# Every second step's second stage in three float32r passes on high and low parts

## The chip, the cores and the metric

The kernel runs on one core of a Trainium2 chip. The metric is the device time of one execution in microseconds (us); three runs of the kernel before gave 1559.08, 1560.92 and 1562.91 us, with the median 1560.92. Profiles are of single executions.

## The reference

The input x has 8 batches of 3136 rows and 256 columns. Each column is filtered over the rows by a real Fourier transform, a product with a complex filter and the transform back. The result goes through a gated feed-forward stage: a product with w_in (256 to 1024), a maximum with zero, a convolution of width 3 along the rows, a sigmoid of it as a gate, and a product with w_out (1024 to 256).

```python
X = np.fft.rfft(x, axis=1)
F = (filt_r + 1j * filt_i)[None, :, :]
y = np.fft.irfft(X * F, n=x.shape[1], axis=1)

h = np.maximum(y @ w_in, 0.0)
...
gate = 1.0 / (1.0 + np.exp(-conv_out))
out = (h * gate @ w_out)
```

## The kernel before

The transform of length 3136 is factored as 112 x 28 and written as matrix products. It is done in steps: 14 steps for each of 8 batches, 112 in all; step number m stands for batch m // 14 and p = m % 14. As 14 is even, p is even where m is even. A step holds two of the 28 sub-transforms, as tiles of about 112 partitions and 2 x 256 elements. What happens to a step, by the functions of the kernel:

- `load` brings x from memory (SyncE's queue), `first` multiplies by s1 on TensorE (8 matmul records, L323), and `keep` copies the result from PSUM into the tile `turn` on ScalarE (L327). These run a whole batch ahead of the rest.
- `turn` transposes a part of the kept tiles on TensorE (L334), and `turned_rows` copies the result `ps` from PSUM to the tile `a` on ScalarE (L339).
- `second` multiplies `a` by s2 on TensorE in plain float32 into `pp` (L346; the last step of a batch in two halves, L349). A float32 matmul shows as two records.
- `filt` multiplies by the filter on VectorE, three instructions that read `pp` from PSUM (L358 to L360), and adds the two products `u` and `v` into `z` on GpSimd (L362).
- `third` multiplies `z` by i1 on TensorE (L233), and `store` copies the result on ScalarE (L237) and writes it to memory.
- `last_stage` and `last_out` read it back, multiply by m2 (L215) and split the result into a high float32r part on ScalarE (`hi_act`, L146) and a low one, the difference, on VectorE (`lo_dve`, L149). For batch 0 this stands at the end of the transform (i from 113); for the others it is spread over the feed-forward stage.

The order of the four compute engines is written out by hand: `manual_schedule` keeps each engine to the order of the code. One iteration i, with m = i - 15, does in this order: `last_out` (late iterations only), `filt(m-2)`, `third(m-4)`, `first(i-1)`, `second(m-1)`, `turn(m)`, `store(m-4)`, `keep(i-1)`, `turned_rows(m)`, `copy_filter` (the first 14 steps), one piece of the weight conversion, `last_stage`. So `a` of step m is written in iteration i, behind `turn(m)`, and read in iteration i + 1, behind `third` and `first`; and on VectorE stands in one iteration `filt(m-2)`, then the conversion.

The weight conversion (`to_f32`, L160 to L174) makes float32 of float64 words for w_in and w_out. From i = 36 on, `next(wsteps)` advances it by one call in each iteration, by two where i is a multiple of 8. Of ten calls, seven issue one VectorE operation between tiles in SBUF (128x512 each), the others work on GpSimd and ScalarE.

PSUM has eight buffers in the transform: five named `ps`, used in turn by `first`, `turn`, `third` and `last_stage`, and three named `pp`. `mm3` (L176 to L179) is the helper for a product in three passes: high x high, high x low, low x high. The feed-forward stage uses it for w_in, and starts when batch 0 is split as a whole.

Of the kernel before, what the change touches and what calls it, by code (L numbers as in the profile page):

```python
# [9 lines left out]
F32 = mybir.dt.float32  # L10
F32R = mybir.dt.float32r
I32 = mybir.dt.int32
U32 = mybir.dt.uint32
AF = mybir.ActivationFunctionType
# [6 lines left out]
D = 256  # L21
# [103 lines left out]
def tile_fft_filter_gated_ffn(  # L125
# [16 lines left out]
    nc = tc.nc  # L142
    B = x.shape[0]

    def hi_act(dst, src):
        nc.scalar.activation(dst, src, AF.Copy)  # L146

    def lo_dve(dst, src, hi):
        nc.vector.tensor_tensor(out=dst, in0=src, in1=hi.bitcast(F32), op=ALU.subtract)  # L149
# [26 lines left out]
    def mm3(ps, wh, wl, rh, rl, start=True, stop=True, **kw):  # L176
        nc.tensor.matmul(ps, lhsT=wh, rhs=rh, start=start, stop=False, **kw)  # L177
        nc.tensor.matmul(ps, lhsT=wh, rhs=rl, start=False, stop=False, **kw)  # L178
        nc.tensor.matmul(ps, lhsT=wl, rhs=rh, start=False, stop=stop, **kw)  # L179
# [16 lines left out]
    def last_load(b, c):  # L196
        br = lp.tile([112, 2, D], F32, name="br", bufs=4)
        nc.sync.dma_start(out=br, in_=b_dram[b][c:c + 2].rearrange("n p d -> p n d"))
        lasts[b, c] = br
# [18 lines left out]
    def last_out(b, c):  # L218
        yh, yl = y_slices(b, slice(c, c + 2))
        pv = lasts.pop((b, c))[:, 0:4 * N1].rearrange("p (k c a) -> p k c a", c=2, a=N1)  # L220
        hi_act(yh, pv)
        lo_dve(yl, pv, yh)

    NP = 14
# [5 lines left out]
    def third(b, p, ps):  # L230
        z = parts.pop((b, p))
        for j in range(2):
            nc.tensor.matmul(ps[:, j], lhsT=i1_sb[:, 2 * p + j], rhs=z[:, j], start=True, stop=True)  # L233

    def store(b, p, ps):
        st = rest.tile([112, 2, D], F32, name="sb")
        nc.scalar.activation(st, ps, AF.Copy)  # L237
        v = b_dram[b].rearrange("n (r g) d -> (n r) g d", g=G)
        nc.scalar.dma_start(out=v[:, 2 * p:2 * p + 2], in_=st)
# [5 lines left out]
    with (  # L245
# [6 lines left out]
        eye_sb = fc.tile([128, 128], F32, name="eye_sb")  # L252
        s2_sb = fc.tile([112, 120], F32, name="s2_sb")
        s2s_sb = fc.tile([112, 120], F32, name="s2s_sb")

        turned = [fc.tile([120, 2, D], F32, name=f"v{k}") for k in range(2)]
        for v in turned:
# [7 lines left out]
        def load_filter(p):  # L265

            sl = slice(2 * p, 2 * p + 2)
            nc.sync.dma_start(out=t2_sb[0:56, sl], in_=fi[0:56, sl])
            nc.sync.dma_start(out=t1_sb[64:120, sl], in_=fr[64:120, sl])
            if p == NP - 1:  # L270
                nc.sync.dma_start(out=t1_sb[0:56, sl], in_=fr[0:56, sl])
            nc.sync.dma_start(out=i1_sb[:, sl], in_=i1[:, sl])

        def copy_filter(p):
            sl = slice(2 * p, 2 * p + 2)
            nc.scalar.activation(t2_sb[64:120, sl], t2_sb[0:56, sl], AF.Copy, scale=-1.0)
            if p < NP - 1:
                nc.vector.tensor_copy(t1_sb[0:56, sl], t1_sb[64:120, sl])
# [38 lines left out]
        def first(b, p):  # L317

            r = rows.pop(("x", b, p))
            ps = fps.tile([128, 512], F32, name="ps")[:, 0:448].rearrange("p (k n m) -> p k n m", k=KT, n=2)  # L320
            for j in range(2):
                for k in range(KT):
                    nc.tensor.matmul(ps[:, k, j], lhsT=r[:, j, 128 * k:128 * k + 128], rhs=s1_sb[:, 2 * p + j], start=True, stop=True)  # L323
            return ps

        def keep(b, p, ps):
            nc.scalar.activation(turns[b % 2][:, :, 2 * p:2 * p + 2], ps, AF.Copy)  # L327

        def turn(b, p):
            ps = fps.tile([112, 2, D], F32, name="ps")  # L330
            for j in range(2):
                for k in range(KT):
                    v = turns[b % 2][:, k].rearrange("p n (r g) -> p (n r) g", g=G)[:, :, 2 * p + j]
                    nc.tensor.transpose(ps[:, j, 128 * k:128 * k + 128], v, eye_sb)  # L334
            return ps

        def turned_rows(b, p, ps):
            r = fp.tile([112, 2, D], F32, name="a", bufs=2)
            nc.scalar.activation(r, ps, AF.Copy)  # L339
            rows["a", b, p] = r  # L340

        def second(b, p):
            r = rows.pop(("a", b, p))
            pp = fps.tile([120, 2, D], F32, name="pp", bufs=3)
            if p < NP - 1:
                nc.tensor.matmul(pp, lhsT=s2_sb, rhs=r, start=True, stop=True)  # L346
            else:
                for j, m in ((0, s2_sb), (1, s2s_sb)):
                    nc.tensor.matmul(pp[:, j], lhsT=m, rhs=r[:, j], start=True, stop=True)  # L349
            psums[b, p] = pp  # L350

        def filt(b, p):


            pp, v = psums.pop((b, p)), turned[p % 2]
            sl = slice(2 * p, 2 * p + 2)
            u = fp.tile([120, 2, D], F32, name="u")
            nc.vector.tensor_mul(u, pp, t1_sb[:, sl])  # L358
            nc.vector.tensor_mul(v[64:120], pp[0:56], t2_sb[0:56, sl])  # L359
            nc.vector.tensor_mul(v[0:56], pp[64:120], t2_sb[64:120, sl])  # L360
            z = rest.tile([120, 2, D], F32, name="z")
            nc.gpsimd.tensor_tensor(out=z, in0=u, in1=v, op=ALU.add)  # L362
            parts[b, p] = z

        def at(i):
            return divmod(i, NP) if 0 <= i < NP * B else None
# [4 lines left out]
        def load_first(i):  # L371
            if i < NP and i % 2 == 0:
                nc.sync.dma_start(out=s1_sb[:, 2 * i:2 * i + 4], in_=s1[:, 2 * i:2 * i + 4])
            if bp := at(i):
                load(*bp)
# [7 lines left out]
        with tc.manual_schedule(engines=COMPUTE):  # L383
            for i in range(NI):
                m = i - SKEW
                if i == done:
                    assert next(wsteps, None) is None
                    convert_pools.close()
                    forward_pools.close()
                    yps.append(ctx.enter_context(tc.tile_pool(name="y_even", bufs=1, side="right", reuse_waits="tile")))  # L390
                    lp = ctx.enter_context(tc.tile_pool(name="lp", bufs=2, side="right", reuse_waits="tile"))
                if i:
                    load_first(i + XBUFS - 1)
                if i == 8:
                    nc.sync.dma_start(out=eye_sb, in_=eye)
                    nc.sync.dma_start(out=s2_sb, in_=s2[:, 0:120])
                    raws["cw"] = cv.tile([128, 6 * NF], I32, name="rawc", bufs=1)
                    nc.sync.dma_start(out=raws["cw"], in_=conv_w)
                if 10 <= i < 10 + NP:
                    load_filter(i - 10)  # L400
                if i == 16:
                    nc.sync.dma_start(out=s2s_sb, in_=s2s[:, 0:120])
                    nc.sync.dma_start(out=m2_sb, in_=m2)
                c = 2 * (i - done)
                if 0 <= c - 4 < N2:
                    last_out(0, c - 4)
                if bp := at(m - 2):
                    filt(*bp)
                pt = None
                if (bp := at(m - 4)) and m - 4 <= END:  # L410
                    pt = fps.tile([112, 2, D], F32, name="ps")
                    third(*bp, pt)
                pf = first(*bp) if (bp := at(i - 1)) else None
                if bp := at(m - 1):
                    second(*bp)
                pa = turn(*bp) if (bp := at(m)) else None
                if pt is not None:
                    store(*at(m - 4), pt)
                if pf is not None:
                    keep(*at(i - 1), pf)  # L420
                if pa is not None:
                    turned_rows(*at(m), pa)
                if 0 <= m - 1 < NP:
                    copy_filter(m - 1)
                if 14 <= i < 22:
                    next(csteps, None)
                if i in (30, 32):
                    load_weights((i - 30) // 2)
                if i >= 36:
                    for _ in range(2 if i % 8 == 0 else 1):  # L430
                        next(wsteps, None)
                if 0 <= c - 2 < N2:
                    last_stage(0, c - 2, fps.tile([128, 512], F32, name="ps"))
                if 0 <= c < N2:
                    last_load(0, c)
# [156 lines left out]
```

## Time and profile before

| | |
|---|---|
| median of three runs | 1560.92 us |
| the profiled execution, its own time | 1562.36 us |
| its span, first to last instruction | 1560.6 us |
| PE busy share | 99% |
| DVE busy share | 83% |
| ACT busy share | 80% |
| POOL busy share | 45% |
| mean granted TensorE clock | 0.999 |
| share of the chain of waits: PE, DVE, DMA, ACT | 92%, 4%, 2%, 1% |

PE is TensorE, PEld its weight loads, DVE VectorE, ACT ScalarE, POOL GpSimd, SP SyncE. A group's row gives the line of the kernel, the engine, the operation, the tile written and those read, the shape, the count, the busy time in us with the mean of one in ns, and behind the last bar the idle time of the engine before such instructions and who ended it. A timeline's row begins with the start and the duration in us; in square brackets stands the idle time before. A row of the chain of waits has start, duration and what was waited for. Matmuls are pipelined: the start of the next one tells what a matmul costs, not its own length.

### The profile page before, as it was taken

Reading aid. Unit: us, or ns where it says so; the run is one execution under the profiler, and the core shown is the slowest. Engines: PE = TensorE matmul, PEld = TensorE weight load, DVE = VectorE, ACT = ScalarE, POOL = GpSimd, SP = SyncE. Lnnn points to the kernel's source line nnn. Section 1 sums busy time; section 2 is a strip of 40 time slices with the busy share of each in tenths; the row PEclk is TensorE's granted clock in tenths of the full one; section 3 lists DMA queues with packets and bytes.
Section 4 is the critical chain, followed back from the end, with each engine's and each line's share of the span. In section 5 each row is a group of like instructions: output and inputs, shape, how many; then the busy total and the mean of one; then the engine's idle time right before and its main releaser. Section 6 shows DMA issues by size and latency. Waiting matters only on the chain.

```text
span 1560.6 us, 27784 instructions
## 1 busy us (share of the span) xinstructions
PE 1539.0 (99%) x10320; PEld 1418.8 (91%) x10320; DVE 1294.3 (83%) x1978; ACT 1245.1 (80%) x2274; POOL 703.9 (45%) x625
## 2 busy tenths in 40 slices
PE   8999999998999999999999999999999999999998
PEld 7778777777999999999999999999999999999998
DVE  3788888788888888888888888888888888888887
ACT  5655555666888888888888888888888888888887
POOL 2455555543444444444444444444444444444444
PEclk9999999999999999999999999999999999999999
DMA  9865655442111011111111011111011110100001
GB/s 228 253 184 165 181 166 162 138 143 88 31 54 48 30 48 48 48 49 48 48 42 34 27 54 48 48 48 48 31 45 46 49 54 26 47 25 24 25 25 48
DMA packets 89062, 115.24 MB, mean 74 GB/s; under 512 B 7400, under 2 KB 60168, under 8 KB 88928
## 3 DMA queue, kind: packets, MB, share of 16 engines
q1 hardware_dynamic: 74592, 87.77, 18.5%
q10 hardware_dynamic: 14336, 25.70, 5.8%
q8 instruction: 82, 1.34, 0.3%
q14 instruction: 52, 0.43, 0.1%
HBM read 62.06 MB, written 51.38 MB: 73 GB/s over the span
## 4 chain that ended last, share of the span: by engine, by line
PE 92%; DVE 4%; DMA 2%; ACT 1%; issue 0%; POOL 0%; SPq 0%; ACTq 0%; POOLq 0%
PE ps_h L178 12%; PE ps_h L179 12%; PE ps_h L177 11%; PE po L494 11%; PE po L496 11%; PE po L495 11%; PE ps_h L215 6%; PE ps L323 5%; PE ps L233 5%; PE pp L346 5%; PE ps L334 2%; DVE y L149 1%; DMA x<-in_x 1%; DVE v L360 1%; DVE v L359 1%; DVE u L358 1%
## 5 line engine op out<-in xcount | busy, mean ns | idle before, releaser
L152 POOL TENSOR_TENSOR g<-t,g 128x448 fp32r<-128x448 f32 x448 | 517.7, 1156 | 663.1 <-ACT g L146 259.6
L494 PE MATMUL po<-wo,g 128*128 128x256 f32 x1568 | 441.5, 282 | 0.0
L496 PE MATMUL po<-wo,g 128*128 128x256 f32 x1568 | 433.8, 277 | 0.0
L495 PE MATMUL po<-wo,g 128*128 128x256 f32 x1568 | 433.4, 276 | 0.0
L468 DVE SCALAR_TENSOR_TENSOR t<-ps_h,cw,t 128x448 f32<-128x448 f32 x448 | 305.5, 682 | 84.6 <-ACT t L463 73.8
L178 PE MATMUL ps_h<-y,wi 128*128 128x450 f32 x896 | 330.4, 369 | 5.2 <-DVE y L149 5.2
L177 PE MATMUL ps_h<-y,wi 128*128 128x450 f32 x896 | 329.1, 367 | 3.9 <-DVE t L474 2.6
L179 PE MATMUL ps_h<-y,wi 128*128 128x450 f32 x896 | 328.8, 367 | 0.0
L469 DVE SCALAR_TENSOR_TENSOR t<-ps_h,cw,t 128x448 f32<-128x448 f32 x448 | 306.4, 684 | 16.0
L463 ACT ACTIVATE t<-ps_h,cw 128x448 f32<-128x448 f32 x448 | 285.2, 637 | 41.5 <-ACT ps_h L461 0.4
L494 PEld LDWEIGHTS po<-wo,g 128*128 128x128 f32 x1568 | 294.8, 188 | 7.0
L495 PEld LDWEIGHTS po<-wo,g 128*128 128x128 f32 x1568 | 294.3, 188 | 5.7
L496 PEld LDWEIGHTS po<-wo,g 128*128 128x128 f32 x1568 | 294.5, 188 | 0.0
L461 ACT ACTIVATE ps_h<-ps_h 128x450 f32<-128x450 f32 x448 | 251.5, 561 | 33.6 <-PE ps_h L179 27.7
L474 DVE TENSOR_TENSOR t<-ps_h,t 128x448 f32<-128x448 f32 x448 | 275.2, 614 | 0.1
L473 ACT ACTIVATE t<-t 128x448 f32<-128x448 f32 x448 | 255.0, 569 | 12.0 <-DVE t L469 10.8
L146 ACT ACTIVATE g<-t 128x448 fp32r<-128x448 f32 x448 | 254.4, 568 | 0.2 <-DVE t L474 0.2
L362 POOL TENSOR_TENSOR z<-u,v 120x512 f32<-120x512 f32 x112 | 156.8, 1400 | 186.2 <-DVE v L360 166.3
L178 PEld LDWEIGHTS ps_h<-y,wi 128*128 128x128 f32 x896 | 168.4, 188 | 14.3 <-DVE y L149 7.5
L177 PEld LDWEIGHTS ps_h<-y,wi 128*128 128x128 f32 x896 | 170.0, 190 | 12.3 <-DVE t L474 3.8
L179 PEld LDWEIGHTS ps_h<-y,wi 128*128 128x128 f32 x896 | 168.3, 188 | 13.9
L149 DVE TENSOR_TENSOR y<-ps_h,y 128x448 fp32r<-128x448 f32 x98 | 103.2, 1053 | 76.9 <-ACT y L146 76.9
(62 smaller groups left out, 1660.9 us busy)
## 6 DMA issues: line engine op xcount, KB each, us to landing
x<-in_x SPq DMA_DIRECT2D x112, 224.0 KB, 3.1
b_dram<-sb ACTq DMA_DIRECT2D x112, 224.0 KB, 3.2
br<-b_dram SPq DMA_DIRECT2D x112, 224.0 KB, 2.6
out<-ot SPq DMA_DIRECT2D x27, 896.0 KB, 4.1
raw<-in_w_in SPq DMA_DIRECT2D x8, 256.0 KB
raw<-in_w_out SPq DMA_DIRECT2D x8, 256.0 KB
t_sb<-in_fr SPq DMA_DIRECT2D x15, 112.0 KB
t_sb<-in_fi SPq DMA_DIRECT2D x14, 112.0 KB
```

The costliest lines, as they stand in the source:

```text
L152: nc.gpsimd.tensor_tensor(out=dst, in0=src, in1=hi.bitcast(F32), op=ALU.subtract)
L177: nc.tensor.matmul(ps, lhsT=wh, rhs=rh, start=start, stop=False, **kw)
L178: nc.tensor.matmul(ps, lhsT=wh, rhs=rl, start=False, stop=False, **kw)
L179: nc.tensor.matmul(ps, lhsT=wl, rhs=rh, start=False, stop=stop, **kw)
L463: nc.scalar.activation(t, h[:, 1:SUB + 1], AF.Copy, scale=cw[:, 1, f:f + 1])
L468: nc.vector.scalar_tensor_tensor(out=t, in0=h[:, 0:SUB], scalar=cw[:, 0, f:f + 1], in1=t, op0=ALU.mult, op1=ALU.add)
L469: nc.vector.scalar_tensor_tensor(out=t, in0=h[:, 2:SUB + 2], scalar=cw[:, 2, f:f + 1], in1=t, op0=ALU.mult, op1=ALU.add)
L473: nc.scalar.activation(t, t, AF.Sigmoid)
L474: nc.vector.tensor_mul(t, h[:, 1:SUB + 1], t)
L494: nc.tensor.matmul(o, lhsT=gh[:, sl], rhs=wo[0][:, f], start=first, stop=False, skip_group_check=True)
L495: nc.tensor.matmul(o, lhsT=gh[:, sl], rhs=wo[1][:, f], start=False, stop=False, skip_group_check=True)
L496: nc.tensor.matmul(o, lhsT=gl[:, sl], rhs=wo[0][:, f], start=False, stop=last, skip_group_check=True)
```

## The change

In even steps ScalarE's copy of the turned rows is replaced by `hi_act`, which writes a float32r tile `a_hi` of the same shape, and VectorE gets a new instruction, `lo_dve`, which writes `a_lo`, the difference of the PSUM tile and `a_hi`. `second` then runs three float32r passes with s2, split in the same way once at i = 12, in place of a float32 matmul. Odd steps keep the float32 form, the last step of a batch (p = 13) with its two halves too. The buffers of `a` are one each of `a`, `a_hi` and `a_lo` in place of two of `a`.

```diff
+        s2_parts = [fc.tile([112, 120], F32R, name=f"s2_{h}") for h in ("hi", "lo")]
...
         def turned_rows(b, p, ps):
-            r = fp.tile([112, 2, D], F32, name="a", bufs=2)
-            nc.scalar.activation(r, ps, AF.Copy)
+            if p % 2:
+                r = fp.tile([112, 2, D], F32, name="a", bufs=1)
+                nc.scalar.activation(r, ps, AF.Copy)
+            else:
+                r = [fp.tile([112, 2, D], F32R, name=f"a_{h}", bufs=1) for h in ("hi", "lo")]
+                hi_act(r[0], ps)
+                lo_dve(r[1], ps, r[0])
             rows["a", b, p] = r
...
-            if p < NP - 1:
+            if p % 2 == 0:
+                mm3(pp, *s2_parts, *r)
+            elif p < NP - 1:
                 nc.tensor.matmul(pp, lhsT=s2_sb, rhs=r, start=True, stop=True)
...
+                if i == 12:
+                    hi_act(s2_parts[0], s2_sb)
+                    lo_dve(s2_parts[1], s2_sb, s2_parts[0])
```

Where the instructions stand now, at three places. In the kernel after the change the lines are shifted: L366 to L368 are the filter's three products, L335 the turn, L324 the first stage, L354 the float32 second stage.

On VectorE, in the iterations with the weight conversion (`em`, `ws` and `raw` are its tiles); before:

```order
L164 TENSOR_TENSOR em<-em 128x512
L358 TENSOR_TENSOR u<-pp,t_sb 120x512
L359 TENSOR_TENSOR v_102<-pp,t_sb 56x512
L360 TENSOR_TENSOR v_102<-pp,t_sb 56x512
L166 TENSOR_SCALAR em<-raw 128x512
L358 TENSOR_TENSOR u<-pp,t_sb 120x512
L359 TENSOR_TENSOR v_103<-pp,t_sb 56x512
L360 TENSOR_TENSOR v_103<-pp,t_sb 56x512
L168 SCALAR_TENSOR_TENSOR ws<-em 128x512
```

The same stretch now:

```order
L164 TENSOR_TENSOR em<-em 128x512
L366 TENSOR_TENSOR u<-pp,t_sb 120x512
L367 TENSOR_TENSOR v_104<-pp,t_sb 56x512
L368 TENSOR_TENSOR v_104<-pp,t_sb 56x512
L149 TENSOR_TENSOR a_lo<-ps,a_hi 112x512
L166 TENSOR_SCALAR em<-raw 128x512
L366 TENSOR_TENSOR u<-pp,t_sb 120x512
L367 TENSOR_TENSOR v_105<-pp,t_sb 56x512
L368 TENSOR_TENSOR v_105<-pp,t_sb 56x512
L168 SCALAR_TENSOR_TENSOR ws<-em 128x512
```

In every second iteration the low part stands between the filter and the conversion; the other iterations are as they were.

On VectorE, in the last iterations of the transform, where batch 0's output is split (`y`); before:

```order
L149 TENSOR_TENSOR y_3322<-ps,y_3321 128x2x2x112
L358 TENSOR_TENSOR u<-pp,t_sb 120x512
L359 TENSOR_TENSOR v_103<-pp,t_sb 56x512
L360 TENSOR_TENSOR v_103<-pp,t_sb 56x512
L149 TENSOR_TENSOR y_3322<-ps,y_3321 128x2x2x112
```

Now:

```order
L367 TENSOR_TENSOR v_104<-pp,t_sb 56x512
L368 TENSOR_TENSOR v_104<-pp,t_sb 56x512
L149 TENSOR_TENSOR a_lo<-ps,a_hi 112x512
L149 TENSOR_TENSOR y_3526<-ps,y_3525 128x2x2x112
L366 TENSOR_TENSOR u<-pp,t_sb 120x512
L367 TENSOR_TENSOR v_105<-pp,t_sb 56x512
L368 TENSOR_TENSOR v_105<-pp,t_sb 56x512
L149 TENSOR_TENSOR y_3526<-ps,y_3525 128x2x2x112
```

Here too a low part follows every second filter, ahead of the next output split.

On TensorE, from one turn to the next but one; before:

```order
L233 MATMUL ps<-z,i_sb 112x256 x2
L323 MATMUL ps<-s_sb,x 128x112 x4
L346 MATMUL pp<-a,s_sb 120x512
L334 MATMUL ps<-eye_sb,turn_97 112x128 x4
L233 MATMUL ps<-z,i_sb 112x256 x2
L323 MATMUL ps<-s_sb,x 128x112 x4
L346 MATMUL pp<-a,s_sb 120x512
```

Now:

```order
L233 MATMUL ps<-z,i_sb 112x256 x2
L324 MATMUL ps<-s_sb,x 128x112 x4
L177 MATMUL pp<-a_hi,s_hi 120x512
L178 MATMUL pp<-a_lo,s_hi 120x512
L179 MATMUL pp<-a_hi,s_lo 120x512
L335 MATMUL ps<-eye_sb,turn_97 112x128 x4
L233 MATMUL ps<-z,i_sb 112x256 x2
L324 MATMUL ps<-s_sb,x 128x112 x4
L354 MATMUL pp<-a,s_sb 120x512
```

Every second float32 matmul has become three instructions; the first reads only `a_hi`, and the second is the first to read `a_lo`.

## The prediction

> **What bounds the kernel now.** I read the busy line of the page first, then the windows by stage, then the chain of waits inside the long stage, and last the rows of the engine that has the least room.
>
> The page, and the windows (PE, PEld, DVE, ACT, POOL busy with counts, granted clock, DMA share, GB/s):
>
> ```profile
> PE 1539.0 (99%) x10320; PEld 1418.8 (91%) x10320; DVE 1294.3 (83%) x1978; ACT 1245.1 (80%) x2274; POOL 703.9 (45%) x625
> ...
> 88.00:305.00 217.00, 217.00 (x1294) 173.09 (x1293) 182.69 (x271) 127.77 (x230) 124.53 (x95) 1.00 0.55 165
> 329.00:369.00 40.00, 38.04 (x227) 30.18 (x225) 38.78 (x53) 25.87 (x37) 15.91 (x13) 1.00 0.50 152
> ```
>
> The change touches only the transform, about the first 370 us of the span. In 88 to 305 us PE is never idle and DVE is busy 84%; in 329 to 369 us DVE is busy 97% and is itself the limit. The chain of waits between 100 and 105 us, one iteration after the other:
>
> ```profile
> 100.00 0.88 PE ps L323 x8
> 100.88 0.87 PE pp L346 x2
> 101.75 0.44 PE ps L334 x4
> 102.19 0.86 PE ps L233 x4
> 103.05 0.88 PE ps L323 x8
> ```
>
> So an iteration is four PE stretches: 0.86 + 0.88 + 0.87 + 0.44 = 3.05 us, with nothing else in the chain. An even step's second stage costs 0.87. I count in pairs of iterations: the odd i, in which an even step is turned and split, and the next, in which its three passes run. A pair takes 6.10 us now.
>
> **PE: what the three passes save.** Consecutive float32r matmuls of the later stage, from the timeline:
>
> ```profile
> 374.82 0.36 PE L177 MATMUL ps_h<-y,wi 128*128 128x450 f32 x1
> 375.02 0.37 PE L178 MATMUL ps_h<-y,wi 128*128 128x450 f32 x1
> ```
>
> They start 0.20 us apart though each is shown 0.36 long, since they are pipelined. With 512 columns in place of 450 that is 0.20 x 512/450 = 0.23, three passes 0.69 to 0.70: **0.17 saved per pair**, which becomes 5.93. The other end, 0.36 each and not pipelined (0.41 at 512 columns, 1.23 in all), would lose 0.36; I take the spacing, which is the nearest row. The Trainium skill ("TensorE: Matmul & The Clock Gate", section "Wait — 56ns, not 53.3ns?") gives a warm matmul N/2.4 ns plus 2.5 ns, by estimate 0.65 for the three and 0.22 saved; the rows above (0.20 for 450, by the rule 0.190) lie a little over it, and by it the sum below would be less by about 1 us.
>
> **DVE: what the split adds.** The groups by line in 88 to 305 us, and the nearest other subtraction, in 329 to 367 us:
>
> ```profile
> L358 DVE TENSOR_TENSOR u<-pp,t_sb 120x512 f32<-120x512 f32 x71 | 49.1, 692 | 29.2 <-PE pp L346 25.2 <-PE pp L349 2.7 <-PE ps L334 0.6
> ...
> L149 DVE TENSOR_TENSOR y<-ps,y 128x448 fp32r<-128x448 f32 x13 | 13.2, 1019 | 2.8 <-ACT y L146 2.4
> ```
>
> The new low part reads one operand from PSUM and one from SBUF, 512 elements, exactly as L358: 0.69, with the gap 0.72. L149 is the same operation but writes every 28th element; scaled to 512 it would be 1.16. I take 0.69, since the new tiles are contiguous, and keep 1.16 as the upper end; the lower end is the same 0.69, for no row of this shape is shorter. ACT's high part takes the place of a copy of the same shape (L339, 0.60), so ACT's work stays. No DMA is added or moved; PE, SP and POOL keep their order but for the passes. The turned rows' PSUM buffer is freed by the low part, 0.7 later, and is used again two iterations on.
>
> **How late the low part may be.** The timeline at 157 us (a is the turned copy), and two rows for the signal from engine to engine:
>
> ```profile
> 157.15 0.60 ACT L339 ACTIVATE a<-ps 112x512 f32<-112x512 f32 x1 [0.66 <-PE ps L334]
> ...
> 158.69 1.03 PE L346 MATMUL pp<-a,s_sb 112*120 112x512 f32 x2
> ...
> 372.26 0.63 ACT L463 ACTIVATE t<-ps_h,cw 128x448 f32<-128x448 f32 x1
> ...
> 372.93 0.68 DVE L468 SCALAR_TENSOR_TENSOR t<-ps_h,cw,t 128x448 f32<-128x448 f32 x1 [1.54 <-ACT t L463]
> ...
> 368.39 0.97 DVE L149 TENSOR_TENSOR y<-ps,y 128x448 fp32r<-128x448 f32 x1
> ...
> 369.42 0.74 PE L178 MATMUL ps_h<-y,wi 128*128 128x450 f32 x1 [1.31 <-DVE y L149]
> ```
>
> High part done at 157.75, DVE starts 0.04 later, ends 158.48, PE may go 0.06 later: 158.54. The second pass would start at 158.69 + 0.23 = 158.92. So a free DVE is in time by **0.38 us**, and a DVE more than that behind holds PE. Before, three pp buffers let DVE lag by about an iteration for nothing; that cover is gone. Queued behind the waiting low part on DVE are the weight conversion and the next filter, and PE's second pass waits for it with the next turn, third and first stages behind.
>
> **What DVE's queue then costs.** Filter and conversion in the same stage:
>
> ```profile
> 156.90 0.43 DVE L170 TENSOR_SCALAR em<-ws 128x512 int32<-128x512 int32 x1
> ...
> 157.35 0.69 DVE L358 TENSOR_TENSOR u<-pp,t_sb 120x512 f32<-120x512 f32 x1
> ...
> 158.78 0.69 DVE L360 TENSOR_TENSOR v<-pp,t_sb 56x512 f32<-56x512 f32 x1
> ...
> 159.50 0.69 DVE L172 SCALAR_TENSOR_TENSOR em<-raw,em 128x512 f32<-128x512 uint32 x1
> 159.64 1.69 POOL L362 TENSOR_TENSOR z<-u,v 120x512 f32<-120x512 f32 x1 [1.19 <-DVE v L360]
> ...
> 160.22 0.69 DVE L358 TENSOR_TENSOR u<-pp,t_sb 120x512 f32<-120x512 f32 x1
> ...
> 149.92 1.69 POOL L362 TENSOR_TENSOR z<-u,v 120x512 f32<-120x512 f32 x1 [1.63 <-DVE v L360]
> ...
> 150.51 1.38 DVE L166 TENSOR_SCALAR em<-raw 128x512 int32<-128x512 int32 x1
> ...
> 125.48 1.41 POOL L362 TENSOR_TENSOR z<-u,v 120x512 f32<-120x512 f32 x1 [1.34 <-DVE v L360]
> ...
> 125.80 1.64 DVE L168 SCALAR_TENSOR_TENSOR ws<-em 128x512 f32<-128x512 int32 x1
> ```
>
> A filter is 159.50 - 157.35 = 2.15. A conversion operation is 0.43 (L160, L162, L166, L170) or 0.69 (L164, L168, L172), (4 x 0.43 + 3 x 0.69)/7 + 0.03 = 0.57 on average with its gap. It now starts 0.03 after the filter, ahead of POOL's z (0.14 after). If z runs first, DVE's operation stays until 0.28 us after z's end (150.51 + 1.38 = 151.89 against 151.61), or 0.55 for the long kind (127.44 against 126.89). That hits today only the second of two conversions in a row. In the changed order the low part stands between filter and conversion: z starts 0.14 after the filter and, at about 1.29 undisturbed, ends at 1.43; the conversion starts at 0.75 and ends at 1.71 or 1.98 in place of 1.18 or 1.44. **Each conversion behind a low part costs 0.51 more.** The low part itself, with one operand from PSUM, I cost without this, as L358 runs beside z at 0.69. The Trainium skill ("SBUF — State Buffer", "Who interferes with whom") says just this of the shared port pair: held for the whole instruction by scalar operations and by two-SBUF-input ones, not by one with a single SBUF input. The rows agree on the first (1.38 for 0.43).
>
> Base of a pair on DVE: 2 x 2.15 + 0.72 = 5.02. From i = 37 to 112 the code has 38 pairs; of ten calls of the conversion seven are DVE operations, and every eighth iteration makes two:
> - 17 pairs with one conversion in each iteration: 5.02 + 0.57 + 0.51 + 0.57 = 6.67;
> - 4 with one, then two (the second 1.5 and its gap, after 1.38 and 1.64 above): 6.67 + 1.53 = 8.20;
> - 4 with one in the first only (always L172): 5.02 + 0.72 + 0.51 = 6.25;
> - 1 with two in the second only: 5.02 + 0.46 + 1.5 = 7.0;
> - 12 with less, left to PE: 5.93.
>
> Sum 113.4 + 32.8 + 25.0 + 7.0 + 71.2 = 249.4, against 38 x 6.10 = 231.8: +17.6. Seven of the runs of such pairs begin after a PE-bound pair, where DVE waits for the high part: there the 0.38 is used up first, and z is over before the conversion (0.51): 7 x 0.89 = -6.2. **88 to 320 us: +11.4.** That DVE's average had room (84%) does not help: the work comes in bursts of seven conversions, and PE cannot get back what it waits.
>
> **The other stretches.** 326 to 371 us: DVE runs without a gap, a filter and an output split per iteration:
>
> ```profile
> 340.64 1.02 DVE L149 TENSOR_TENSOR y<-ps,y 128x448 fp32r<-128x448 f32 x1
> 340.79 1.29 POOL L362 TENSOR_TENSOR z<-u,v 120x512 f32<-120x512 f32 x1 [1.80 <-DVE v L360]
> ...
> 343.74 1.01 DVE L149 TENSOR_TENSOR y<-ps,y 128x448 fp32r<-128x448 f32 x1
> ```
>
> 3.10 us an iteration against PE's 3.05, and the gated stage starts only when the last of them is done (369.42 above). Six low parts fall here (steps 100 to 110): 6 x 0.72 = **+4.3**, with no gain from PE. Before 88 us, DVE's waits, and the loads in PE's chain of waits:
>
> ```profile
> 55.93 0.42 DVE L278 COPY t_sb<-t_sb 56x512 f32<-56x512 f32 x1 [1.83 <-DMA t_sb<-in_fr]
> ...
> 62.85 0.42 DVE L278 COPY t_sb<-t_sb 56x512 f32<-56x512 f32 x1 [1.63 <-DMA t_sb<-in_fr]
> ...
> 77.45 0.69 DVE L358 TENSOR_TENSOR u<-pp,t_sb 120x512 f32<-120x512 f32 x1 [0.92 <-PE pp L346]
> ```
>
> ```profile
> 59.90 4.72 DMA x<-in_x
> ...
> 66.81 5.36 DMA x<-in_x
> ...
> 72.31 1.12 PE ps L323 x8
> ```
>
> Seven low parts here, with the filter copies pushed into z as above, cost DVE 7 x (0.72 + 0.5) = 8.5; it had 1.8 and 1.6 us of waits for loads (first rows), and PE's own two load waits of 5 us each end after DVE would, so I book nothing, and +3 as the other end. From 72 to 88 us DVE idles 0.9 in each iteration (the row at 77.45), which covers the low part: three pairs, -0.5, and one more before 326 us, -0.2. The two parts of s2 are 112x120, once, while PE waits for loads.
>
> **Sum:** 11.4 + 4.3 - 0.5 - 0.2 = +15.0, on the profiled execution's 1562.4 (span 1560.6 and 1.8 around it) 1577.4. That execution stood 1.4 over the median of 1560.9; on the median 1575.9. Forecast **1576**, about 1% slower.
>
> **Rivals.** A difference of 0.3%, 4.7 us, is about what a measurement of this kernel can tell.
> - *The cover holds and PE's gain stays* (faster). DVE idles 34 us in 88 to 305 us and needs 36 x 0.72 = 26 more. Its place is the 0.38 us of slack: if DVE's lag stayed under it, 49 pairs from 72 us on would give 49 x -0.17 = -8.3: 1553. Against it: with two conversions a pair DVE needs 6.16 even without collisions, over 5.93, and 326 to 371 us has no idle DVE at all. Chance 0.08.
> - *DVE bounds, but conversions don't meet z*, because the low part mostly waits for its high part first. Then 17 x 6.16 + 4 x 7.69 + 7.0 + 16 x 5.93 = 237.4, +5.6, less 7 x 0.38 = +2.9; with the other stretches +6.5: 1567. Chance 0.14.
> - *The low part costs as L149* (1.16): 0.47 x (26 pairs + 6) = +15 more: 1591. The strided output speaks against it. Chance 0.10.
> - *The passes don't pipeline* (the change doesn't save PE time): the 15 pairs left to PE at 5.93 + 0.53, +8 more: 1584. Chance 0.06.
>
> **How the numbers follow.** My forecast has 0.62, with 1569 to 1584 by itself (the count of collisions, the start of the run, the early loads). The range reaches down to the no-collision case and up towards a dear low part: 1563 to 1590. Faster by over 0.3% is the first rival, 0.08; within 0.3% is the lower half of the second, 0.08; slower 0.84.
>
> **What would show it.** Right: in 88 to 305 us PE's idle time put down to DVE's a_lo, 0.4 to 0.8 us in most pairs, DVE's share near 95%, the conversion after a low part at 0.96 or 1.23, the low part at 0.69; passes 0.23 apart; y splits 3.1 and 3.8 us apart by turns after 329 us; the stage after 371 us unchanged but later. Wrong: PE still gapless in the long stage, or a low part over 1 us, or the later start not coming from these two stretches.

## The result, and the profile after

The changed kernel takes 1579.11 us, the median of five runs (1575.02 to 1579.65), against 1560.36 of the kernel before in five runs (1558.98 to 1562.91): a ratio of **1.0104, 95% interval 1.0091 to 1.0117**, about 16 us slower. The two medians lie 18.8 us apart, just outside that interval, and the two profiled executions 16.7; I go by the ratio. The forecast was 1576 with 1563 to 1590.

The busy line of the page after, and the windows of the two stages (PE, PEld, DVE, ACT, POOL busy with counts, granted clock, DMA share, GB/s):

```profile
PE 1539.3 (98%) x10376; PEld 1430.9 (91%) x10376; DVE 1330.3 (84%) x2035; ACT 1244.4 (79%) x2275; POOL 707.8 (45%) x625
...
88.00:305.00 217.00, 208.49 (x1273) 173.31 (x1272) 194.96 (x292) 121.68 (x219) 122.35 (x89) 1.00 0.53 160
...
329.00:369.00 40.00, 36.72 (x221) 29.33 (x220) 36.28 (x51) 23.80 (x36) 15.33 (x16) 1.00 0.47 139
```

TensorE, gapless before in 88 to 305 us, now idles 8.5 us there, and VectorE is busy 195 us in place of 183. The granted clock in these windows is the same, 1.00.

Where the time came from is best read from one instruction that both kernels have once a step: the filter's first product (L358 before, L366 now). Its starts in the timeline of the kernel after, for steps 18, 96 and 111:

```profile
85.75 0.69 DVE L366 TENSOR_TENSOR u<-pp,t_sb 120x512 f32<-120x512 f32 x1
...
332.42 0.69 DVE L366 TENSOR_TENSOR u<-pp,t_sb 120x512 f32<-120x512 f32 x1
...
384.31 0.68 DVE L366 TENSOR_TENSOR u<-pp,t_sb 120x512 f32<-120x512 f32 x1
```

Before they stood at 83.55, 321.54 and 369.28. So the delay is 2.2 us up to step 18 (the early stage), grows by **8.7** up to step 96 (the long stage) and by **4.1** up to step 111 (the output stage). The spans differ by 16.7; the last 1.7 us came after step 111, 1.2 of them in the gated stage at a lower granted clock (last section). In the long stage, 88 to 320 us, who waited for whom (total us, times, longest):

```profile
DVE a_lo L149 <- ACT a_hi L146: 17.8, 23, 3.2
...
PE ps L233 <- POOL z L370: 3.5, 9, 0.6
PE pp L178 <- DVE a_lo L149: 3.5, 6, 0.9
...
PE pp L177 <- ACT a_hi L146: 1.2, 1, 1.2
```

TensorE waits as long for z at the third stage as for the low part at the second; and VectorE itself stands 17.8 us at the low part until the high part is there. The low part's own group, and the three passes in the chain of waits:

```profile
L149 DVE TENSOR_TENSOR a_lo<-ps,a_hi 112x512 fp32r<-112x512 f32 x37 | 25.6, 692 | 18.2 <-ACT a_hi L146 17.8
```

```profile
78.14 0.24 PE pp L177
78.38 0.23 PE pp L178
78.61 0.23 PE pp L179
```

These two terms are as forecast: 0.692 us, and 0.70 for the passes.

The output stage, in the chain of waits, one pair of iterations:

```profile
355.64 0.70 DVE a_lo L149
356.35 0.04 issue
356.39 0.49 PE pp L178
356.88 0.23 PE pp L179
357.12 0.44 PE ps L335 x4
357.55 0.89 PE ps L215 x8
...
358.47 1.00 ACT y L146
...
359.50 1.03 DVE y L149
360.53 0.59 DVE u L366
361.14 0.69 DVE v L367
...
361.86 0.69 DVE v L368
...
362.58 0.70 DVE a_lo L149
```

Here the low part is in a loop: the second pass follows it by 0.05 us, and turn, last stage, output split and filter lead to the next low part. The pair takes 362.58 - 355.64 = 6.94 us; before, a pair took 6.16 us, twice the 3.08 from one output split to the next.

### The profile page after: what moved, and what is told of

Same layout as the page of the kernel before. It is cut to its first block, busy times and chain, and to the rows that moved or that the text cites. A ratio compares the mean times of both kernels' runs of the same rounds, so it can differ in the third digit from the quotient of the medians.

```text
span 1577.3 us, 27904 instructions
## 1 busy us (share of the span) xinstructions
PE 1539.3 (98%) x10376; PEld 1430.9 (91%) x10376; DVE 1330.3 (84%) x2035; ACT 1244.4 (79%) x2275; POOL 707.8 (45%) x625
## 4 chain that ended last, share of the span: by engine, by line
PE 85%; DVE 8%; POOL 2%; ACT 2%; DMA 1%; issue 1%; ACTq 0%; SPq 0%; POOLq 0%; DVEq 0%
PE ps_h L178 12%; PE ps_h L179 12%; PE ps_h L177 11%; PE po L505 11%; PE po L507 11%; PE po L506 11%; PE ps_h L215 5%; PE ps L233 3%; PE ps L324 3%; POOL z L370 2%; PE ps L335 2%; DVE v L368 2%; DVE v L367 2%; DVE u L366 1%; PE pp L354 1%; DVE a_lo L149 1%
## 5 line engine op out<-in xcount | busy, mean ns | idle before, releaser
L484 ACT ACTIVATE t<-t 128x448 f32<-128x448 f32 x448 | 255.0, 569 | 11.9 <-DVE t L480 10.8
L370 POOL TENSOR_TENSOR z<-u,v 120x512 f32<-120x512 f32 x112 | 161.3, 1440 | 197.7 <-DVE v L368 179.3
L149 DVE TENSOR_TENSOR y<-ps_h,y 128x448 fp32r<-128x448 f32 x98 | 103.3, 1054 | 77.4 <-ACT y L146 77.4
```

The source lines that it names most:

```text
L484: nc.scalar.activation(t, t, AF.Sigmoid)
```

## The experiments

Theory: VectorE's queue carries the cost. Rivals: the float32r passes cost TensorE time; VectorE has simply too much work; the collisions with GpSimd. Each run has a profile and was timed beside the kernel before. The last three columns are the changes of the delay of the filter's first product against the kernel before, in one profile each. The rows with a star are kernels with the second stage one iteration later. Their filter runs one iteration later too, so that steps 18 to 96 would take in the iteration behind the last first stage, which is shorter by that stage's 0.88 us. Their two columns are read from ScalarE's copy of the turned rows instead, steps 19 to 97 and 97 to 111, which every kernel has in the same iteration; by it the change has +8.7 and +5.4.

| kernel | ratio to before, 95% interval | early | long stage | output stage |
|---|---|---|---|---|
| the change | 1.0104 (1.0091 to 1.0117) | +2.2 | +8.7 | +4.1 |
| split unused | 1.0115 (1.0101 to 1.0130) | +2.2 | +13.2 | +2.8 |
| no low part | 0.9955 (0.9943 to 0.9967) | -2.4 | -6.2 | -0.2 |
| second one later* | 1.0045 (1.0033 to 1.0057) | | +6.3 | +2.8 |
| no conversion | 0.9998 (0.9990 to 1.0007) | -2.4 | -4.6 | +4.2 |
| low after conversion | 1.0080 (1.0063 to 1.0098) | +1.1 | +3.5 | +4.2 |
| low in next iteration* | 1.0026 (1.0016 to 1.0037) | | +1.9 | +2.7 |
| last batch float32 | 1.0070 (1.0053 to 1.0088) | +0.1 | +8.7 | -0.9 |
| first batch float32 | 1.0083 (1.0065 to 1.0101) | -1.9 | +8.6 | +4.1 |
| spread alone | 1.0050 (1.0038 to 1.0062) | 0.0 | +1.1 | +4.1 |
| next iteration and spread* | 0.9971 (0.9961 to 0.9981) | | -6.2 | +2.8 |
| that, inner batches only* | 1.0057 (1.0045 to 1.0069) | | -6.2 | +14.9 |
| before, spread | 1.0003 (0.9994 to 1.0011) | +0.3 | 0.0 | -0.1 |

The long stage repeats to 0.1 us where its code is the same (8.7, 8.7, 8.6); the early stage does not (+2.2, +0.1 and 0.0 with the same code up to there, and -2.4 without the conversion, which up to there leaves out only the few small operations for the convolution's weights).

### The split alone, unused

```diff
             r = fp.tile([112, 2, D], F32, name="a", bufs=2)
             nc.scalar.activation(r, ps, AF.Copy)
+            if p % 2 == 0:
+                lo = fp.tile([112, 2, D], F32, name="a_lo", bufs=1)
+                nc.vector.tensor_tensor(out=lo, in0=ps, in1=r, op=ALU.subtract)
```

> Every second stage runs in float32 again from the copy of the turned rows; in even steps VectorE still subtracts the copy from PSUM into a tile that nothing reads. So VectorE has the change's extra work in the same place of its queue, and TensorE neither waits for it nor gains. Theory (VectorE's queue carries the cost, and TensorE's wait with 0.38 us of slack turns its bursts into lost time): before 72 us and after 329 us the loss of the changed kernel stays (+2.3 and +5 to +6), in 88 to 320 us the three pp buffers cover the lag again and nearly nothing is lost (0 to +3): 1567 to 1572 us. Rival (the float32r passes and their weight loads on TensorE cost the time): 1560 to 1562 us. Second rival (VectorE is simply full in the long stage, cover or not): 1576 us or more.

Measured: 1.0115, 18 us, the second rival's side and not my theory's 6 to 11. The long stage loses 13.2 us though TensorE never waits for this low part. The change loses 8.7 there after a gain of 6.2 (next run), 14.9 in all, so that most of it needs no reader of the low part. The chain of waits shows how:

```profile
100.69 0.60 ACT a L340
101.30 0.02 issue
101.32 0.69 DVE a_lo L343
102.01 0.86 DVE em L166
102.87 0.60 DVE u L362
...
103.48 0.68 DVE v L363
...
104.18 0.70 DVE v L364
...
104.91 0.70 DVE ws L168
...
105.63 0.04 DVE em L170
105.67 1.38 issue
107.05 0.69 DVE u L362
...
109.33 2.29 POOL z L366
...
111.67 1.12 PE ps L233 x4
```

VectorE's low part is tied to this iteration's turn and copy; conversion, filter, two conversions and the next filter queue behind it, then z, and TensorE waits for that z at the third stage. The second of the two conversions, 0.43 us by itself, took 1.39 here with z of the filter before beside it; the kernel before has the same 1.38. The three `pp` buffers don't cover it, since it is not the second stage that runs dry.

### The passes alone, without a low part

```diff
-                r = [fp.tile([112, 2, D], F32R, name=f"a_{h}", bufs=1) for h in ("hi", "lo")]
+                r = [fp.tile([112, 2, D], F32R, name="a_hi", bufs=1)] * 2
                 hi_act(r[0], ps)
-                lo_dve(r[1], ps, r[0])
```

> Three float32r passes in even steps, but the second pass takes the high part where the changed kernel takes the low part, and no low part of the rows is made: its share of the product is replaced. TensorE has exactly the changed kernel's work, VectorE that of the kernel before. Theory: TensorE saves 0.17 us in each of 49 pairs after 72 us where it is the bound: 1552 to 1554 us. Rival (the passes cost TensorE as much as the float32 product or more): 1560 us or more.

Measured: 0.9955, 7 us faster, the theory's side (8.3 forecast). The passes save 6.2 us from step 18 to 96, 39 pairs at 0.16, with TensorE gapless. The rival that the passes cost time is out.

### Second stage one iteration later

```diff
-                if bp := at(m - 1):
+                if bp := at(m - 2):
                     second(*bp)
```

`filt`, `third` and `store` are shifted by one in the same way.

> The changed kernel with second, filter, third and store one iteration later against turn, so that the low part may be late by one iteration (some 3.3 us in place of 0.38). VectorE's work and its order by kind stay. Theory: VectorE's bursts in 88 to 320 us are evened out, with 226 to 230 us of work against 225 us of TensorE's: that stage goes from +8.7 to between -5 and 0, the early and the last stage stay: 1565 to 1571 us. Rival (VectorE's work as such, or its collisions with GpSimd, are the price): 1576 to 1580 us as the changed kernel.

Measured: 1.0045, within the theory's range, but with the long stage at +6.3 and not below 0. An iteration of room gives back 2.4 us there. TensorE no longer waits for the low part at all, but 8.0 us for z at the third stage; VectorE still stands 15.4 us at the low part for its high part.

### Without the conversion on VectorE

```diff
         pairs = raw.rearrange("p (n t) -> p n t", t=2)
-        low, high = pairs[:, :, 0].bitcast(U32), pairs[:, :, 1]
-        v.tensor_scalar(e, high, 3, 0x3FFFFFF8, op0=ALU.logical_shift_left, op1=ALU.bitwise_and)
-        yield
...
-        nc.gpsimd.tensor_tensor(out=dst, in0=dst, in1=e.bitcast(F32), op=ALU.add)
+        high = pairs[:, :, 1].bitcast(F32)
+        for _ in range(7):
+            yield
+        nc.gpsimd.tensor_tensor(out=dst, in0=high, in1=high, op=ALU.add)
```

> The changed kernel without VectorE's conversion of the weights: the seven VectorE operations of each round are left out, one addition on GpSimd remains, so that the weights are wrong numbers. Theory: without the bursts the 88 to 320 us stretch is TensorE's, 0.17 us less in each of 38 pairs: 1579 - 8.7 - 6.5 = 1562 to 1566 us, with the early and the last stage as in the changed kernel. Rival (the split costs by its place alone, whatever else VectorE does): 1575 to 1579 us.

Measured: 0.9998; the long stage gains 4.6 us, of the 6.2 that the passes save. With no conversion beside it the split is mostly covered there, although VectorE now stands 41.8 us at the low part for its high part, more than twice as long as in the change: that wait alone is not the price. The output stage loses its 4.2 as before.

### The low part after the conversion

```diff
+                if lows:
+                    lo_dve(*lows.pop())
                 if 0 <= c - 2 < N2:
                     last_stage(0, c - 2, fps.tile([128, 512], F32, name="ps"))
```

> The changed kernel with the low part put behind the iteration's conversion operation (and behind the filter's copy in the early steps) in VectorE's queue; nothing else moves. Theory (the price in 88 to 320 us is VectorE standing at the low part for its high part, 17.8 us in all, with the conversion and the next filter queued behind it, and z on GpSimd kept out by a conversion that follows the low part at once, 2.0 to 2.4 us in place of 1.3): the conversion fills the waiting time and z comes as before, so that 3 to 7 us of the 8.7 return: 1571 to 1576 us. Rival (VectorE's amount of work sets the time, order does not matter): 1578 to 1580 us. Second rival (the low part, now 0.5 to 0.7 us later, makes TensorE wait more): 1582 us or more.

Measured: 1.0080; the long stage loses 3.5 in place of 8.7, with the same work on VectorE. Its wait for the high part there:

```profile
DVE a_lo L149 <- ACT a_hi L146: 10.8, 9, 3.2
```

10.8 in place of 17.8; TensorE itself waits longer for the low part, 5.9 us in place of 3.5. So the order matters with the amount of work unchanged. How much of this is the waiting and how much z's delay by conversions (below), this run does not separate, since it changes both.

### The low part at the head of the next iteration

```diff
+                if lows:
+                    lo_dve(*lows.pop())
                 if bp := at(m - 3):
                     filt(*bp)
```

On top of the second stage one iteration later.

> As the run with second, filter, third and store one iteration later, and the low part moved to the head of the next iteration on VectorE, so that VectorE never stands waiting for the high part and TensorE still has most of an iteration before it reads the low part. VectorE's work is the same. Theory (waiting in order, not the amount of work): 88 to 320 us loses nothing or gains up to 6 us, the early and the output stage lose what they lost: 1560 to 1566 us. Rival (amount of work): 1569 us, as with the later second stage alone, or more.

Measured: 1.0026, long stage +1.9: of the 6.3 of the later second stage another 4.4 are gone by place alone. The theory's range for the whole time held (4 us over the kernel before); the long stage lost 1.9 where it expected no loss.

### Last batch and first batch in float32

```diff
-            if p % 2:
+            if p % 2 or b == B - 1:
```

and `b == 0` in the other run; `second` has the same condition.

> The changed kernel with the last batch's second stage in float32, as before the change: the seven low parts from step 98 on are gone, so that none falls beside the output splits of batch 0. Theory (that stage is VectorE's, each low part there costs its 0.72 us and more): the 4.6 to 5 us lost there return, 1573 to 1575 us. Rival (the gated stage's start is set by something else): 1578 to 1580 us.

> The changed kernel with the first batch's second stage in float32: no low part falls into the load-bound stretch before 72 us. My prediction booked nothing there, the profile shows 2.3 us lost by step 16. Theory (the copy behind a low part waits for z there, 0.97 us in place of 0.42, and VectorE is the bound): 2 to 3 us return, 1575.5 to 1577 us. Rival (the loads set that stretch, and what is lost there is made up later): 1578.5 to 1580 us.

Measured: without low parts in the last batch the output stage loses nothing (-0.9 in place of +4.1, ratio 1.0070), so its price is theirs. Without those of the first batch the ratio is 1.0083, but its interval overlaps that of the change, and the early stage of equal code differs by 2 us from profile to profile: whether the early low parts cost their 2 us stays open.

### No two conversion operations in one iteration

```diff
-                    for _ in range(2 if i % 8 == 0 else 1):
+                    for _ in range(2 if (i - 36) % 9 == 8 else 1):
                         next(wsteps, None)
```

Now the doubled calls are the one on ScalarE and the one on GpSimd that end a round. The conversion ends in iteration 107, one later than in the change.

> The changed kernel with one thing altered: an iteration takes two calls of the weight conversion only where they are ScalarE's and GpSimd's, so that no iteration has two conversion operations on VectorE (the prediction counted four pairs at 8.20 us and one at 7.0). The same operations in all, ended at the same iteration. Theory (bursts without cover): the excess of those pairs over one-operation pairs, some 6 us, returns, 1571 to 1575 us. Rival (the sum of VectorE's work counts, not its bunching): 1578 to 1580 us.

Measured: 1.0050, and the long stage +1.1: **7.6 of its 8.7 us went with the regrouped calls.** More than I expected of it. Where they had been shows in the changed kernel pair by pair, from ScalarE's copy in one even step to that in the next, against the same pair before. The five pairs behind an iteration with two conversion operations lose 1.2 to 1.9 us each, 7.4 in all. One more pair, with iteration 96 in it, loses 2.3. The two calls of that iteration are GpSimd's addition and ScalarE's split of the weights: ScalarE waits for GpSimd, and VectorE at the next low part for ScalarE.

```profile
284.75 0.42 ACT L146 ACTIVATE wi<-ws 128x256 fp32r<-128x256 f32 x1 [3.22 <-POOL ws L174]
...
287.41 0.69 DVE L149 TENSOR_TENSOR a_lo<-ps,a_hi 112x512 fp32r<-112x512 f32 x1 [3.19 <-ACT a_hi L146]
```

All other pairs together gain 0.9. With the calls regrouped no pair loses more than 0.54. The windows of this run:

```profile
88.00:305.00 217.00, 214.16 (x1317) 179.54 (x1316) 198.19 (x305) 126.36 (x226) 126.13 (x91) 1.00 0.56 166
```

TensorE idles 2.8 us in place of 8.5, 2.4 of it waiting for z and none for the low part, with VectorE further on in its work in the same time; VectorE still stands 15.9 us at the low part. The regrouping takes away more than the bunches, though. The second of two conversion operations had stretched beside z to 1.38 to 1.64 us in each of the five; the 56 operations together now take 4.6 us less. How much of the 7.6 is the bunch and how much this collision with z is not separated. Control, on the kernel before:

> The kernel before the change with the same spreading of the conversion alone, as a control: TensorE is the bound there and VectorE's bunches are covered, so both theories expect no difference, 1559 to 1562 us. If it were faster by itself, the gain of the two runs before would have to be lessened by it.

Measured: 1.0003. There the bunches had been covered, and the collisions too.

### Both, and both in the inner batches only

The first run is the kernel with the low part at the head of the next iteration (and the second stage one later), with the condition `(i - 36) % 9 == 8` as well.

> The low part at the head of the next iteration, with the second stage one iteration later, and in addition no iteration with two conversion operations. Theory: with neither waits in order nor bunches TensorE is the bound through 88 to 320 us and keeps its 0.17 us a pair, so that stage goes from about +1 to between -3 and -6; the early and the output stage stay: 1559 to 1562 us. Rival (a pair of 5.9 to 6.2 us of VectorE's work holds it): 1564 to 1566 us, as without the spreading.

Measured: **0.9971 (0.9961 to 0.9981), 1556.8 us: faster than both kernels,** and better than the theory's 1559 to 1562. The windows:

```profile
88.00:305.00 217.00, 217.00 (x1361) 184.14 (x1360) 205.88 (x313) 130.94 (x235) 129.24 (x97) 1.00 0.56 168
```

TensorE is gapless again with VectorE at 95%; the long stage gains 6.2 us, all that the passes saved there in the run without a low part, and the output stage loses 2.8, where the change loses 5.4 by the same copy.

The second of the two runs leaves the outer batches in float32:

```diff
-            if p % 2:
+            if p % 2 or b in (0, B - 1):
                 r = fp.tile([112, 2, D], F32, name="a", bufs=1)
...
-            if p % 2 == 0:
+            if p % 2 == 0 and not (b in (0, B - 1)):
                 mm3(pp, *s2_parts, *r)
```

> The same, with the first and the last batch's second stage in float32, so that low parts are made only where TensorE is the bound. Theory: 42 even steps left, each 0.17 us, and no loss before 72 us and after 329 us: 1553 to 1557 us, faster than the kernel before by 0.3 to 0.5%. Rival (what is left in the long stage takes the gain): 1559 us or more.

Measured: 1.0057, a miss by an oversight of the edit. In the float32 batches every step now uses the one buffer `a`, and with the second stage one iteration later the copy of a step waits until the step before has been multiplied. The waits from 320 to 385 us:

```profile
ACT a L342 <- PE pp L355: 28.3, 13, 4.0
```

So the output stage loses 14.9. The long stage (-6.2) is as in the run before; float32 in the outer batches with two buffers was not tried.

## Why the prediction was right, point by point

The total, its sign and the two stages were right: +15.0 forecast on the profiled execution, 16.7 between the spans. That the total came so near is in part luck: the long stage was booked 2.0 too high (11.4 less 0.7, against 8.7), and 2.2 in the early stage and 1.7 behind step 111, booked at nothing, made up for it. By its own steps:

- *The passes, 0.17 a pair*: right. 0.70 in the rows, 0.16 a pair in the run without a low part.
- *The low part, 0.69, not as dear as L149*: right, 0.692.
- *Output stage, +4.3*: right in size, 4.1, and the run with the last batch in float32 takes it away. Its form was nearly so: I wrote VectorE without a gap, and the loop passes through TensorE and ScalarE too (6.94 a pair, where 2 x 3.08 + 0.72 would be 6.88; VectorE idles 0.2 us of it). The output splits are 3.69 and 3.25 us apart by turns, for 3.8 and 3.1.
- *Early stage, 0*: 2.2 in the profile, within the +3 that I gave as the other end, but not settled by the runs.
- *Long stage, +11.4 less 0.7*: 8.7. The size is near; of the working, three parts need mending. Three of the signs named for it did not come: VectorE's share is 90% (194.96 of 217 us) and not near 95%, TensorE waits for the low part in 6 pairs of 37 and not in most, and no conversion behind a low part takes 0.96 or 1.23.

First, **"PE's second pass waits" and the 0.38 us of slack as the place.** TensorE does wait there (6 times, 3.5 us), but the split that nobody reads costs 13.2 in the same stage, and a second stage one iteration later, which ends that wait, gives back only 2.4. The place is VectorE's own queue: the low part waits for this iteration's turn, and what stands behind it reaches TensorE by way of z. The cover that was lost is not that of the `pp` buffers.

Second, **"Each conversion behind a low part costs 0.51 more."** (From the rows beside it, 1.71 - 1.18, it would be 0.53.) Not in the long stage. The timeline of the change where the low part follows the filter at once:

```profile
108.29 0.69 DVE L149 TENSOR_TENSOR a_lo<-ps,a_hi 112x512 fp32r<-112x512 f32 x1
...
108.43 2.29 POOL L370 TENSOR_TENSOR z<-u,v 120x512 f32<-120x512 f32 x1 [2.60 <-DVE v L368]
108.90 0.68 DVE L172 SCALAR_TENSOR_TENSOR em<-raw,em 128x512 f32<-128x512 uint32 x1
```

The conversion ran in 0.68 and z took 2.29. So it was in all 12 low parts there that z had not preceded and a conversion followed: conversions 0.42 or 0.68, z 2.02 to 2.42. In the other 13, where VectorE had waited for the high part and z had begun before, the conversions took 0.51 to 0.84. So these were stretched by up to 0.4, but the 0.96 and 1.23 of my sum do not occur in the long stage. In the early stage the shorter one does, for the filter's copy:

```profile
51.57 0.69 DVE L149 TENSOR_TENSOR a_lo<-ps,a_hi 112x512 fp32r<-112x512 f32 x1
...
51.71 1.28 POOL L370 TENSOR_TENSOR z<-u,v 120x512 f32<-120x512 f32 x1 [1.30 <-PE ps L233]
...
52.30 0.98 DVE L279 COPY t_sb<-t_sb 56x512 f32<-56x512 f32 x1
```

Third, **the weights within the sum.** I put 17 x 0.57 = 9.7 us on the pairs with one conversion in each iteration and 8.4 + 0.9 on the five with two in one, less 6.2 and less what TensorE gains. Measured pair by pair, the five with two and the pairs right behind them carry 7.5, near my 9.3. The 13 other pairs with one conversion in each iteration gain 0.4 together: they were booked too dear, which fits the second error, though no run takes the collisions out by themselves. The 2.3 of the pair with iteration 96 is not in my sum. That bursts decide, and not VectorE's average, was right.

The rival with the cover that holds, 1553, was a question of order: with the low part at the head of the next iteration, the second stage one later and the conversions spread, the long stage keeps all that the passes save there, 6.2 us in 39 pairs (the rival's 8.3 counts 49).

## What to carry to other kernels

An instruction put into an in-order engine's queue brings its own wait with it: what stands behind it is then tied to whatever it waits for, even if nobody needs its result soon. The wait costs nothing while little stands behind it (41.8 us of it in the run without conversions) and much where work is bunched there; so put the instruction where its input has long been there, here at the head of the next iteration. An engine at 84% on average had no room for more work here, since the work came in bunches that the buffers didn't cover: spread the bunches first, which by itself changed nothing in the kernel before and was worth some 8 us after the change (1.0104 against 1.0050). To see where such a change costs, follow one instruction that both traces have once a step.

## What the hardware showed that was not expected

GpSimd's z, shown as started 0.47 to 0.60 us before a conversion on VectorE, was stretched from 1.28 to as much as 2.42 us when the conversion followed a low part directly, at 0.61 us after its start, while the conversion kept its 0.42 or 0.68. In all 12 cases z ended 1.13 to 1.16 us after the conversion's end, as if it had begun its work only then. Yet the copy at 0.73 us after a low part's start waited for z (0.98 for 0.42). The Trainium skill ("SBUF — State Buffer", "Who interferes with whom") lets whoever issues first hold the shared port pair for the whole instruction. The copy agrees with that; the 12 stretched z don't, if their shown start is their issue. GpSimd's spans are rough, and what decides between the two was not isolated.

The granted clock of TensorE differs between executions at the start of the gated stage, where TensorE works between waits. The same stretch of work in the kernel before and after the change (PE, PEld, DVE, ACT, POOL busy with counts, granted clock, DMA share, GB/s):

```profile
382.00:390.00 8.00, 6.49 (x42) 5.84 (x41) 7.21 (x12) 7.63 (x17) 4.03 (x4) 1.00 0.03 11
```

```profile
397.00:405.00 8.00, 6.21 (x29) 5.46 (x28) 6.66 (x11) 7.59 (x16) 3.45 (x4) 0.79 0.07 20
```

Across these some 15 us the delay grows by 0.0 us in four of the thirteen other profiles, by 1.1 to 1.3 in six and by 2.5 in three, though their code is the same there; the windows of the first group show 1.00, of the second 0.79 and of the third 0.57 to 0.66. So a single profile's span can be off by 2.5 us for this reason alone, and a stage is better compared by its own delay. What decides about the clock there stays open.
